# Mish from one Tanh and a polynomial instead of exponentials and reciprocals, and 56 instead of 47 sets of attention exponentials on VectorE

## The chip, the cores and the metric

The kernel runs on one core of one Trainium2 chip. A core has several engines that run at the same time, each with its own list of instructions: PE (TensorE, matrix products, with weight loads shown as PEld), ACT (ScalarE, tables of functions such as exp), DVE (VectorE, elementwise work), POOL (GpSimd) and SP (SyncE, which here only issues DMAs). An engine takes its instructions in order and waits at one until the semaphores that it needs are there.

The metric is the time of one execution on the device, in microseconds. Before the change the median of three runs is 902.22 us (902.0 to 902.47).

## What is computed

The input x has 2048 rows of 640. Two branches are mixed by a gate for each row: attention with 32 heads of 20 columns, and an MLP with the activation Mish.

```python
qkv = x @ wqkv                        # q, k, v: 32 heads of 20
scores = einsum("bhqd,bhkd->bhqk", q, k) * Dh ** -0.5
a = softmax(scores) @ v               # then @ wo
h = einsum("bsd,df->bsf", x, w1) + b1           # 640 -> 1536
sp = log1p(exp(-abs(h))) + where(h > 0, h, 0)   # softplus
b = einsum("bsf,fd->bsd", h * tanh(sp), w2)     # Mish, then 1536 -> 640
g = sigmoid((x * gate_w).sum(-1))
out = g * a + (1 - g) * b
```

The MLP takes x itself, as the attention does. Everything comes and goes as bf16.

## The kernel before

**Tiling.** The 2048 rows are four chunks `qc` of 512 queries, and the 32 heads are eight `p` of four heads each. A group G is one (p, qc): 32 groups in all, in the order of the list `groups`. In each group the keys are 16 tiles of 128. For a tile of keys and one head, PE makes a block of scores, 128 keys by 512 queries, in PSUM (L1150, tile `Sp`). The exponential of the block goes to SBUF (L1165, tile `E`), and a second product with the values adds it into `acc` (L1225), four heads at a time. One such step over four heads is called a set; a group has 16 sets. A column of ones beside the values gives the sum of the softmax, so that a group ends with a transpose, a reciprocal and a scaling on VectorE (`normalise`, L1185 to L1202).

**Iterations.** The blocks are handled in iterations that alternate between two score buffers: `S0` holds three blocks of 512 columns and `S1` two. One ACTIVATE takes the exponential of all the blocks in a buffer, so it has 1536 or 1024 columns. There are 819 iterations.

**Sets on VectorE.** Part of the sets have their exponential on VectorE. In such a case the third block of an `S0` buffer belongs to a VectorE set: `jv_read` (L794) rounds the block to int16 in one of the three ring buffers `E_dve`, and the ACTIVATE of that iteration takes only the 1024 columns left. After four such reads, one for each head, `jv_steps` makes the exponential of the set by seven steps on 128x2048 (L810 to L832): bits split into mantissa and exponent, a polynomial and an integer addition. The product for the set then reads `E_dve` and `VB`, a scaled copy of the last two tiles of values. `JV_SETS` says how many sets each group has on VectorE: two in the even groups and in group 31, one in the other groups from 1 on, 47 in all. `blocks` holds the place at which each read should come; within a group the reads are spread evenly.

**Mish.** `h_chain` makes `h` for one tile of 128 MLP columns and one chunk (L660, with the bias added at L670). For two tiles together (`mish_steps`, 24 times) ScalarE takes e = exp(h) (L589), and VectorE computes h * n / (n + 2) with n = e (e + 2). The division takes two fp32 reciprocals of 128x128 (L609) for 1024 columns: products of two and of four denominators are inverted and multiplied back (L599 to L618).

**What sets the order.** All instructions are written out in a fixed order by a planner in the kernel, which keeps estimates of each engine's time (`T`). Work other than scores, exponentials and set products is cut into chains with a start and a due iteration: projections of q, k and v, the MLP, the output projection (`wo_chain`, L739) and bounds that decide whether a fallback with maxima is needed. `pump` puts pieces of the chains between the scores of one iteration and those of the next, and fills PE with products of a constant (`busy_matmul`, L1090) where there is nothing else. VectorE's steps of Mish, of its sets and of `normalise` wait in the list `slow`, each with a deadline, and `run_slow` takes them by that deadline and avoids, where it can, two dependent steps behind each other.

**Ends of the groups.** Heads of pairs 0 to 5 are written to memory and fetched again (`fetch`) shortly before the output projection of their chunk. The last eight groups are, by chunk, pair 6 and pair 7. When pair 7 of a chunk is done, that chunk's output projection starts within the next group. Tiles of MLP activations and of heads share 40 buffers of 128x512 (`cells`).

SP issues the loads of w1, the weight strips and the heads; POOL issues the first loads and pads the q and k weights.

Of the kernel before, what the change touches and what calls it, by code (L numbers as in the profile page):

```python
# [2 lines left out]

# [147 lines left out]
def kernel(  # L151
# [12 lines left out]
    nc = tc.nc  # L164
    _, S, D = A_x.shape
# [7 lines left out]
    QC = 512  # L173
    NQC = S // QC
    NU = QC // P
    NQ = H // 4
# [2 lines left out]
    Q_SCALE = 512.0 * float(DH) ** -0.5 / LN2  # L179
    WIDTHS = (3, 2)  # L180

    JV_TWO = (*range(2, 31, 2), 31)
    JV_SETS = {G: 2 if G in JV_TWO else 1 for G in range(1, 32)}
    JV_RING = 3
    JV_AHEAD = 0.9
    JV_BIAS = 32
    N_CAP = 16382.0
    NCELL = 40
    MLP_FROM, MLP_TO = 10, 1
    CELLS_KEPT = 2  # L190

# [5 lines left out]
    consts = ctx.enter_context(tc.tile_pool(name="consts", bufs=1))  # L197
# [13 lines left out]
    mp = ctx.enter_context(tc.tile_pool(name="mp", bufs=1))  # L211
# [16 lines left out]
    cells = [consts.tile([P, QC], BF16, tag=f"cell{i}", name=f"cell{i}") for i in range(NCELL)]  # L228
    busy = consts.tile([P, P], BF16, tag="busy")
    xn = consts.tile([P, NQC], F32, tag="xn")  # L230
    wn = consts.tile([P, NQ, 2], F32, tag="wn")
    vn = consts.tile([P, 3], F32, tag="vn")
    F16, I16 = mybir.dt.float16, mybir.dt.int16
# [39 lines left out]
    warm = xn[:, 0:1]  # L273
    nc.vector.memset(warm, 0.0)
    nc.vector.memset(busy, 1.0)
    nc.scalar.activation(warm, warm, ACT.Exp)
    for t in (wqp[0], wkp[0], VA[:, :, :, DH : DH + 1], wqp[1], wkp[1], T2):
        nc.vector.memset(t, 1.0 if len(t.shape) == 4 and t.shape[-1] == 1 else 0.0)
    nc.gpsimd.dma_start(out=wv0[:, :, :], in_=wrows[:, :, 2 * D : 2 * D + 4 * DH])
    for c in range(1, NQC):  # L280
        nc.gpsimd.dma_start(
            out=xs[c][:, :, :],
            in_=x2d[c * QC : (c + 1) * QC, :].rearrange("(u p) d -> p u d", p=P),
# [4 lines left out]
        out=wv[:, :, GC : GC + 1], in_=gate_w.rearrange("(kt p o) -> p kt o", p=P, o=1)  # L288
# [14 lines left out]


    groups = [(p, qc) for p in range(NQ - 2) for qc in range(NQC)]
    groups += [(p, qc) for qc in range(NQC) for p in (NQ - 2, NQ - 1)]
    first = {}
    for G, (p, qc) in enumerate(groups):
        first.setdefault(p, G)


    units = []
# [6 lines left out]
    JV_START = {G: G - JV_AHEAD for G in range(34)}  # L319
    JV_START.update({1: 0.95, 25: 24.85, 32: 31.1})  # L320
    blocks = deque(
        (JV_START[G] + b * min(1.0, JV_START[G + 1] - JV_START[G]) / n, G, k, c)
        for G in JV_SETS
        for n in (4 * JV_SETS[G],)
        for b, (k, c) in enumerate((k, c) for k in range(JV_SETS[G]) for c in range(4))
    )
# [6 lines left out]
    while pos < len(units):  # L333
        i = len(iters)
        G = units[pos][0]
        n = min(WIDTHS[i % len(WIDTHS)], len(units) - pos)
        x = None
        far = G + (pos - unit_at[(G, 0)]) / (4.0 * (NS - JV_SETS.get(G, 0)))
        if n == 3 and blocks and blocks[0][0] <= far:
            _, g, k, slot = blocks[0]  # L340
# [3 lines left out]
            if left:  # L344
# [3 lines left out]
                n = 2  # L348
# [10 lines left out]
    def it_at(G, j=0):  # L359
        return it_of[unit_at[(G, j)]] if G < len(groups) else NI  # L360
# [218 lines left out]
    def mish_steps(m, c):  # L579


        h = h_of.pop((m, c))
        mish_free[0] = False
        e = mp.tile([P, 2 * QC], F32, tag="e", name="e")
        d = mp.tile([P, 4, 2 * P], F16, tag="d", name="d")
        d2 = mp.tile([P, 2, 2 * P], F32, tag="d2", name="d2")
        d4 = mp.tile([P, 2 * P], F32, tag="d4", name="d4")
        r2 = mp.tile([P, 2, 2 * P], BF16, tag="r2", name="r2")
        nc.scalar.activation(e[:, :], h[:, :, :].rearrange("p a n -> p (a n)"), ACT.Exp)  # L589
        T["act"] += NS_MISH_EXP  # L590
        V = nc.vector
        r = d2.rearrange("p a n -> p (a n)").bitcast(F16)
        y = d.rearrange("p a n -> p (a n)").bitcast(BF16)

        def n():
            V.scalar_tensor_tensor(out=e, in0=e, scalar=2.0, in1=e, op0=ALU.add, op1=ALU.mult)

        def products():
            V.tensor_scalar(  # L599
                out=d.rearrange("p a n -> p (a n)"), in0=e, scalar1=N_CAP, scalar2=2.0,  # L600
                op0=ALU.min, op1=ALU.add,
            )
            V.tensor_tensor(out=d2, in0=d[:, 0:2, :], in1=d[:, 2:4, :], op=ALU.mult)

        def invert(half):
            cols = slice(half * P, (half + 1) * P)
            if half == 0:
                V.tensor_tensor(out=d4, in0=d2[:, 0, :], in1=d2[:, 1, :], op=ALU.mult)
            V.reciprocal(out=d4[:, cols], in_=d4[:, cols])  # L609

        def of_two():
            V.tensor_tensor(
                out=r2, in0=d2[:, ::-1, :], in1=d4.unsqueeze(1).to_broadcast([P, 2, 2 * P]),
                op=ALU.mult,
            )

        def of_one():
            V.tensor_tensor(  # L618
                out=r.rearrange("p (b a n) -> p b a n", b=2, a=2),
                in0=d.rearrange("p (b a) n -> p b a n", b=2)[:, ::-1, :, :],  # L620
                in1=r2.unsqueeze(1).to_broadcast([P, 2, 2, 2 * P]),
                op=ALU.mult,
            )

        def share():
            V.scalar_tensor_tensor(out=y, in0=e, scalar=N_CAP, in1=r, op0=ALU.min, op1=ALU.mult)
            mish_free[0] = True

        def last(half):
            ft = 2 * m + half  # L630
            t = taken.pop((ft, c))
            V.tensor_tensor(out=t, in0=h[:, half, :], in1=y[:, half * QC : (half + 1) * QC], op=ALU.mult)
            act[(ft, c)] = t
            in_mish[0] -= half

        steps(
            T["act"] + 250.0,
            [
                (1217, n, True), (1415, products, True), (1400, lambda: invert(0), True),
                (947, lambda: invert(1), False), (692, of_two, True), (692, of_one, True),  # L640
                (1222, share, True), (420, lambda: last(0), True), (420, lambda: last(1), False),
            ],
            T["act"] + MISH_DUE,
            "mish",
        )
# [669 lines left out]
    half = QC // 2  # L1315
# [88 lines left out]
    for u in range(NU):  # L1404
        s = NU * last_qc + u
        ps = spool.tile([P, 2, QC], F32, tag=f"S{u % 2}", name="po")
        for half in range(2):
            nc.tensor.matmul(
                ps[:, half, 0:HALF],
                lhsT=OT[(NQ - 1, last_qc)][:, u * P : (u + 1) * P],  # L1410
                rhs=wo_sb[0][:, NQ - 1, half * HALF : (half + 1) * HALF],
                start=True,
                stop=True,
            )
        if u == 0:
            pair = mp.tile([P, 2, 2 * QC], BF16, tag="e", name="ot")
        if u < 2:
            ot = pair[:, u, :]
        else:
            ot = mp.tile([P, 2 * QC], BF16, tag=("d", "d2")[u - 2], name="ot")  # L1420
# [50 lines left out]
```

## Time and profile before

| | |
|---|---|
| median of three runs | 902.22 us |
| profiled execution, its time / its span | 902.6 / 900.8 us |
| ScalarE busy | 878.0 us, 97% |
| PE busy | 820.8 us, 91% |
| VectorE busy | 794.3 us, 88% |
| exponentials on ScalarE (L1165) | 819: 597 of 1024 and 222 of 1536 columns |
| reads of scores by VectorE (L794) | 188, 685 ns each |
| Mish exponentials on ScalarE (L589) | 24, 1142 ns each |
| granted clock of TensorE, mean | 0.996 |

The busy time of a group is the union of its instructions, so that it can be less than the number times the mean: neighbours overlap at their ends. Matmuls are pipelined, and a busy PE isn't PE at its peak. A group's line ends with the idle time of the engine just before its instructions, and with what ended that time (the releaser). "issue" is time in which the engine waited for nothing that the profile shows.

### The profile page before, as it was taken

How to read it: one execution, taken by the hardware profiler on the slowest of the kernel's cores; microseconds unless marked ns; L12 is line 12 of the kernel's file. 1: busy time of each engine (PE TensorE's matmuls, PEld its weight loads, DVE VectorE, ACT ScalarE, POOL GpSimd, SP SyncE). 2: the span in 40 equal slices, each digit the busy share in tenths (PEclk: the TensorE clock that was granted, in tenths of full speed). 3: DMA queues.
4: the chain of work that ended last, by engine and by line, in shares of the span. 5: the costliest groups of instructions: out<-in, count | busy, mean ns of one | idle time of the engine just before them, and what ended most of it. 6: DMA issues, size and time to landing. Idle time of an engine off the chain costs nothing.

```text
span 900.8 us, 14880 instructions
## 1 busy us (share of the span) xinstructions
PE 820.8 (91%) x5993; PEld 297.1 (33%) x6081; DVE 794.3 (88%) x1207; ACT 878.0 (97%) x849; POOL 25.3 (3%) x39
## 2 busy tenths in 40 slices
PE   8999898999998998989999989998999988999996
PEld 4443333233333333333333332333333333333332
DVE  4499999989989999989998999999999999988784
ACT  6999999999999999999999999999999999999994
POOL 5000010000000000000100000000000000000000
PEclk9999999999999999999999999999999999999998
DMA  9100010001000001000102000100001001110111
GB/s 264 36 7 22 21 31 1 21 22 31 7 21 15 21 7 30 22 19 32 31 28 51 8 21 15 31 36 21 21 16 43 27 1 40 44 44 8 50 53 39
DMA packets 37730, 28.27 MB, mean 31 GB/s; under 512 B 10984, under 2 KB 36472, under 8 KB 37656
## 3 DMA queue, kind: packets, MB, share of 16 engines
q1 hardware_dynamic: 34968, 20.90, 8.0%
q0 software_dynamic: 1456, 5.62, 2.1%
q8 instruction: 48, 0.79, 0.4%
q10 hardware_dynamic: 1232, 0.76, 0.3%
q14 instruction: 26, 0.21, 0.1%
HBM read 18.88 MB, written 8.39 MB: 30 GB/s over the span
## 4 chain that ended last, share of the span: by engine, by line
ACT 70%; PE 17%; issue 11%; DVE 2%; DMA 0%; ACTq 0%
ACT E L1165 67%; PE Sp L1150 5%; PE acc L1225 3%; ACT e L589 2%; PE ps L739 2%; PE ps L693 2%; PE ps L522 1%; PE ps L550 1%; PE ps L879 1%; DVE ot L1421 0%; DMA xs<-in_A_x_dram 0%; PE ps L660 0%; PE ps L480 0%; PE ps L1090 0%; PE ps L1301 0%
## 5 line engine op out<-in xcount | busy, mean ns | idle before, releaser
L1165 ACT ACTIVATE E<-Sp 128x1024 bf16<-128x1024 f32 (+1 forms) x819 | 856.6, 1232 | 3.9 <-PE Sp L1150 1.9
L1150 PE MATMUL Sp<-qT,kT 32*128 32x512 bf16 x2048 | 323.0, 382 | 61.5 <-ACT E L1165 44.7
L1150 PEld LDWEIGHTS <-kT 32*128 32x128 bf16 x2048 | 108.2, 91 | 284.6 <-issue 234.4
L1225 PE MATMUL acc<-E,VA 128*21 128x512 bf16 x1860 | 183.8, 386 | 0.0
L794 DVE TENSOR_SCALAR E_dve<-Sp 128x512 int16<-128x512 f32 x188 | 128.7, 685 | 31.7 <-PE Sp L1150 29.9
L1225 PEld LDWEIGHTS <-VA 128*21 128x21 bf16 x1860 | 45.6, 88 | 102.6 <-issue 102.4
L693 PE MATMUL ps<-w_sb,cell 128*128 128x320 bf16 x384 | 76.0, 303 | 0.2 <-issue 0.2
L1090 PE MATMUL ps<-busy 128*128 128x512 bf16 x229 | 71.2, 384 | 1.8 <-issue 1.6
L660 PE MATMUL ps<-xT,w1t 128*128 128x512 bf16 x215 | 71.2, 385 | 1.3 <-issue 1.3
L829 DVE TENSOR_TENSOR w_dve<-w_dve,u_dve 128x2048 bf16<-128x2048 f16 x47 | 57.1, 1215 | 0.2
L832 DVE TENSOR_TENSOR E_dve<-E_dve,w_dve 128x2048 int16<-128x2048 int16 x47 | 57.1, 1215 | 0.2
L820 DVE TENSOR_TENSOR w_dve<-w_dve 128x2048 f16<-128x2048 f16 x47 | 56.9, 1211 | 0.0
L739 PE MATMUL ps<-wo_sb,cell 128*128 128x320 bf16 x248 | 47.9, 302 | 0.0
L522 PE MATMUL ps<-xT,wkp 128*128 128x512 bf16 x135 | 43.3, 384 | 2.4 <-issue 1.4
L522 PE MATMUL ps<-xT,wqp 128*128 128x512 bf16 x137 | 43.9, 384 | 1.1 <-issue 0.9
L609 DVE RECIPROCAL d<-d 128x128 f32<-128x128 f32 x48 | 43.8, 934 | 0.8
L693 PEld LDWEIGHTS <-cell 128*128 128x128 bf16 x384 | 29.1, 97 | 35.4 <-issue 29.5
L670 DVE TENSOR_SCALAR h<-ps,b1f 128x512 bf16<-128x512 f32 x48 | 35.1, 731 | 0.8 <-PE ps L660 0.5
L810 DVE TENSOR_SCALAR w_dve<-E_dve 128x2048 int16<-128x2048 int16 x47 | 32.5, 692 | 1.2
L550 PE MATMUL ps<-wv,xT 128*128 128x80 bf16 (+2 forms) x240 | 33.3, 258 | 0.3 <-DVE xT L488 0.3
L815 DVE TENSOR_SCALAR E_dve<-E_dve 128x2048 int16<-128x2048 int16 x47 | 32.2, 686 | 1.1
L826 DVE TENSOR_SCALAR w_dve<-w_dve 128x2048 f16<-128x2048 f16 x47 | 32.1, 684 | 0.8
(105 smaller groups left out, 608.0 us busy)
## 6 DMA issues: line engine op xcount, KB each, us to landing
w1t<-in_B_w_dram SPq DMA_DIRECT2D x22, 320.0 KB, 3.1
heads_dram<-cell SPq DMA_DIRECT2D x24, 128.0 KB, 1.7
cell<-heads_dram SPq DMA_DIRECT2D x24, 128.0 KB, 2.9
b_dram<-Bt SPq DMA_DIRECT2D x4, 640.0 KB, 3.2
out_dram<-ot SPq DMA_DIRECT2D x14, 160.0 KB, 1.8
xs<-in_A_x_dram POOLq DMA_DIRECT2D x3, 640.0 KB, 7.1
w_sb<-in_B_w_dram POOLq DMA_DIRECT2D x1, 1920.0 KB, 12.6
ws<-in_A_wqkv_dram SPq DMA_DIRECT2D x13, 100.0 KB, 3.0
```

The lines of the kernel that those rows point to most:

```text
L522: nc.tensor.matmul(box["ps"][:, :], lhsT=wpad[:, kt, :, :].rearrange("p h d -> p (h d)"), rhs=xT[:, kt, chunk * QC : (chunk + 1) * QC], st ...
L660: nc.tensor.matmul(box["ps"][:, :], lhsT=w1t[NPAIR * c + m][:, kt, half * P : (half + 1) * P], rhs=xT[:, kt, c * QC : (c + 1) * QC], start ...
L693: nc.tensor.matmul(box["ps"][:, :], lhsT=act[(ft, c)][:, u * P : (u + 1) * P], rhs=w2_sb[:, ft, half * HALF : (half + 1) * HALF], start=(f ...
L739: nc.tensor.matmul(box["ps"][:, :], lhsT=OT[(p, c)][:, u * P : (u + 1) * P], rhs=wo_sb[0][:, p, cols], start=(k == 0), stop=(k == len(ps_l ...
L794: S_reader[0] = nc.vector.tensor_scalar(out=E_dve[ring].bitcast(I16)[:, slot, :], in0=ps, scalar1=ROUND, scalar2=ROUND - 512.0 * JV_BIAS, ...
L820: V.tensor_tensor(out=w, in0=w, in1=w, op=ALU.mult)
L829: V.tensor_tensor(out=w.bitcast(BF16), in0=w, in1=u, op=ALU.mult)
L832: V.tensor_tensor(out=e, in0=e, in1=wi, op=ALU.add)
L1090: nc.tensor.matmul(ps[:, 0:n], lhsT=busy[:, :], rhs=busy_row(n), start=True, stop=True)
L1150: nc.tensor.matmul(ps[:, k * QC : (k + 1) * QC], lhsT=kT[p][32 * t : 32 * t + 32, j * P : (j + 1) * P], rhs=qT[G][32 * t : 32 * t + 32, :] ...
L1165: exp = nc.scalar.activation(E[:, 0 : n * QC], S_of.pop(i)[:, 0 : n * QC], ACT.Exp, scale=LN2 / 512.0)
L1225: nc.tensor.matmul(acc[32 * t : 32 * t + DH + 1, :], lhsT=v, rhs=e, start=(n == 0), stop=(n == NS - 1), tile_position=(0, 32 * t),)
```

## The change

Four things are changed.

1. Mish: ScalarE takes T = tanh(h/2 + c) with c = log(0.4238062491)/2 from the tile `shift_t`, which VectorE fills once at the start. VectorE computes with S = T + 1: v = (S + A) S, then v * ((v + B)^2 + C) * K, all in fp16, and the product with h as before. Eleven VectorE instructions per pair of tiles become nine, and the reciprocals are gone. The planner's costs of the steps are changed with them.
2. VectorE has 56 sets instead of 47. They have one constant length, from place 0.95 to place 31.1 in units of groups, instead of one or two per group spread within it; a set belongs to the group that holds its end less 0.25. Group 1 has none, groups 5, 12, 19 and 26 have one each and the other groups to 31 two.
3. The last eight groups: pairs 6 and 7 of chunks 0 and 1 come as 6, 6, 7, 7, and those of chunks 2 and 3 chunk by chunk as before. The keys of pair 7 are projected over a longer stretch.
4. `cells` has 41 buffers instead of 40.

```diff
-    JV_TWO = (*range(2, 31, 2), 31)
-    JV_SETS = {G: 2 if G in JV_TWO else 1 for G in range(1, 32)}
+    JV_N, JV_FROM, JV_TO, JV_LATE = 56, 0.95, 31.1, 0.25
     JV_RING = 3
-    JV_AHEAD = 0.9
-    N_CAP = 16382.0
-    NCELL = 40
+    MISH_Z, MISH_A, MISH_B, MISH_C, MISH_K = (
+        0.4238062491, -3.9772710648, 1.0644427153, -50.2157789339, 0.00604176076620
+    )
+    NCELL = 41
...
+    nc.vector.memset(shift_t, math.log(MISH_Z) / 2)
...
-    groups += [(p, qc) for qc in range(NQC) for p in (NQ - 2, NQ - 1)]
+    groups += [(NQ - 2, 0), (NQ - 2, 1), (NQ - 1, 0), (NQ - 1, 1)]
+    groups += [(p, qc) for qc in range(2, NQC) for p in (NQ - 2, NQ - 1)]
...
+    set_length = (JV_TO - JV_FROM) / JV_N
+    JV_SETS = {}
+    blocks = deque()
+    for n in range(JV_N):
+        t = JV_FROM + n * set_length
+        G = min(max(1, math.ceil(t + set_length - JV_LATE)), len(groups) - 1)
+        k = JV_SETS.get(G, 0)
+        JV_SETS[G] = k + 1
+        t = max(t, G - 1.0)
+        blocks.extend((t + c * set_length / 4, G, k, c) for c in range(4))
...
-        nc.scalar.activation(e[:, :], h[:, :, :].rearrange("p a n -> p (a n)"), ACT.Exp)
+        nc.scalar.activation(
+            e[:, :], h[:, :, :].rearrange("p a n -> p (a n)"), ACT.Tanh, bias=shift_t[:, 0:1], scale=0.5
+        )
...
+        def one_more():
+            V.tensor_scalar(out=S, in0=e, scalar1=1.0, scalar2=None, op0=ALU.add)
+        def factor():
+            V.tensor_scalar(out=u, in0=S, scalar1=MISH_A, scalar2=None, op0=ALU.add)
+        def product():
+            V.tensor_tensor(out=v, in0=u, in1=S, op=ALU.mult)
+        def shifted():
+            V.tensor_scalar(out=u, in0=v, scalar1=MISH_B, scalar2=None, op0=ALU.add)
+        def square():
+            V.tensor_tensor(out=u, in0=u, in1=u, op=ALU.mult)
+        def factor2():
+            V.tensor_scalar(out=u, in0=u, scalar1=MISH_C, scalar2=MISH_K, op0=ALU.add, op1=ALU.mult)
+        def ratio():
+            V.tensor_tensor(out=S, in0=v, in1=u, op=ALU.mult)
...
-                (1217, n, True), (1415, products, True), (1400, lambda: invert(0), True),
-                (947, lambda: invert(1), False), (692, of_two, True), (692, of_one, True),
-                (1222, share, True), (420, lambda: last(0), True), (420, lambda: last(1), False),
+                (690, one_more, True), (427, factor, True), (692, product, True), (427, shifted, True),
+                (692, square, True), (427, factor2, True), (692, ratio, True),
+                (420, lambda: last(0), True), (420, lambda: last(1), False),
...
         if p == NQ - 1:
-            a, b = it_at(first[p] - 1) + 1, it_at(first[p]) - 4
+            a = it_at(first[p - 1]) + 1
```

More of the change, by code (lines that the diff above doesn't have):

```diff
@@ L1 @@
+import math
 from collections import deque
@@ L230 @@
     xn = consts.tile([P, NQC], F32, tag="xn")
+    shift_t = consts.tile([P, 1], F32, tag="shift_t")
     wn = consts.tile([P, NQ, 2], F32, tag="wn")
@@ L309 @@
         first.setdefault(p, G)
+    set_length = (JV_TO - JV_FROM) / JV_N
[8 more added lines that the diff above has]
+        blocks.extend((t + c * set_length / 4, G, k, c) for c in range(4))
+    assert max(JV_SETS.values()) <= 2
     units = []
@@ L318 @@
             units.extend((G, groups[G][0], groups[G][1], j, (j + k) % 4) for k in range(4))
[L319 to L326, printed above, removed]
     heads_of = {(G, k): [] for G in JV_SETS for k in range(JV_SETS[G])}
@@ L584, in mish_steps @@
         e = mp.tile([P, 2 * QC], F32, tag="e", name="e")
[L585 to L589, printed above, removed]
+        S = mp.tile([P, 2 * QC], F16, tag="y", name="S")
+        nc.scalar.activation(
+            e[:, :], h[:, :, :].rearrange("p a n -> p (a n)"), ACT.Tanh, bias=shift_t[:, 0:1], scale=0.5
+        )
@@ L590, in mish_steps @@
         T["act"] += NS_MISH_EXP
         V = nc.vector
[L592 to L623, printed above, removed]
@@ L625, in share @@
-        def share():
-            V.scalar_tensor_tensor(out=y, in0=e, scalar=N_CAP, in1=r, op0=ALU.min, op1=ALU.mult)
+        u, v = (e.bitcast(F16)[:, k * 2 * QC : (k + 1) * 2 * QC] for k in range(2))
+        def one_more():
[4 more added lines that the diff above has]
+            V.tensor_tensor(out=v, in0=u, in1=S, op=ALU.mult)
@@ L631, in last @@
             t = taken.pop((ft, c))
-            V.tensor_tensor(out=t, in0=h[:, half, :], in1=y[:, half * QC : (half + 1) * QC], op=ALU.mult)
+            V.tensor_tensor(out=t, in0=h[:, half, :], in1=S[:, half * QC : (half + 1) * QC], op=ALU.mult)
             act[(ft, c)] = t
@@ L1419 @@
         else:
-            ot = mp.tile([P, 2 * QC], BF16, tag=("d", "d2")[u - 2], name="ot")
+            ot = mp.tile([P, 2 * QC], BF16, tag=("d", "y")[u - 2], name="ot")
         nc.vector.scalar_tensor_tensor(
```

## The prediction

> **What bounds the kernel now.** I read the busy shares first, then the stages by window, then the groups of ScalarE and VectorE with shapes kept apart, then the waits, and the chain of work that ended last at the end of the span.
>
> The head of the page, and ScalarE and VectorE by stage. The columns of a window are its length, then busy us and count of PE, PEld, DVE, ACT, POOL, then the granted clock, DMA share and GB/s:
>
> ```profile
> span 900.8 us, 14880 instructions
> PE 820.8 (91%) x5993; PEld 297.1 (33%) x6081; DVE 794.3 (88%) x1207; ACT 878.0 (97%) x849; POOL 25.3 (3%) x39
> ...
> 100.00:200.00 100.00, 90.37 (x640) 31.58 (x648) 94.87 (x144) 99.90 (x100) 5.12 (x6) 1.00 0.07 20
> 300.00:400.00 100.00, 90.84 (x643) 32.22 (x652) 94.34 (x139) 100.00 (x98) 0.00 (x0) 1.00 0.06 17
> 600.00:700.00 100.00, 91.01 (x644) 30.95 (x653) 93.02 (x135) 100.00 (x98) 0.72 (x2) 1.00 0.08 23
> 800.00:880.00 80.00, 79.38 (x608) 29.55 (x606) 63.27 (x94) 78.78 (x75) 0.00 (x0) 1.00 0.12 38
> ```
>
> ScalarE (ACT) is busy 100 us of 100 in the middle: the kernel goes at its pace. VectorE is the next, 93 to 95. From 800 us on VectorE has room (63 of 80), but PE is as full as ScalarE.
>
> The groups by shape (busy, mean ns of one, idle before and its releaser):
>
> ```profile
> L1165 ACT ACTIVATE E<-Sp 128x1024 bf16<-128x1024 f32 x597 | 597.4, 1116 | 2.9 <-PE Sp L1150 1.0 <-PE acc L1225 0.3 <-ACT E L1165 0.2
> L1165 ACT ACTIVATE E<-Sp 128x1536 bf16<-128x1536 f32 x222 | 342.5, 1543 | 1.0 <-PE Sp L1150 0.8
> L794 DVE TENSOR_SCALAR E_dve<-Sp 128x512 int16<-128x512 f32 x188 | 128.7, 685 | 31.7 <-PE Sp L1150 29.9
> L820 DVE TENSOR_TENSOR w_dve<-w_dve 128x2048 f16<-128x2048 f16 x47 | 56.9, 1211 | 0.0
> L609 DVE RECIPROCAL d<-d 128x128 f32<-128x128 f32 x48 | 43.8, 934 | 0.8
> L826 DVE TENSOR_SCALAR w_dve<-w_dve 128x2048 f16<-128x2048 f16 x47 | 32.1, 684 | 0.8
> L596 DVE SCALAR_TENSOR_TENSOR e<-e 128x1024 f32<-128x1024 f32 x24 | 29.2, 1218 | 1.7 <-ACT e L589 1.7
> L589 ACT ACTIVATE e<-h 128x1024 f32<-128x1024 bf16 x24 | 27.4, 1142 | 0.2 <-DVE d L626 0.2
> L599 DVE TENSOR_SCALAR d<-e 128x1024 f16<-128x1024 f32 x24 | 16.7, 694 | 0.1
> L618 DVE TENSOR_TENSOR d<-d,r 128x1024 f16<-128x1024 f16 x24 | 16.5, 686 | 0.4
> ```
>
> An exponential of 1536 columns costs 1543 - 1116 = 427 ns more than one of 1024; the third 512 columns are what VectorE takes off ScalarE when it reads a block itself (L794). The 24 Mish exponentials are 3% of ScalarE. VectorE's reads wait for PE, 29.9 us in all, so VectorE still has slack there.
>
> The chain of work that ended last, at its end (start, us, what):
>
> ```profile
> 842.38 0.54 PE ps L739 x4
> 842.93 0.32 PE Sp L1150 x2
> 843.25 0.33 PE acc L1225 x4
> ```
>
> Between about 798 and 845 us this chain goes from score to score over PE, not over ScalarE: the output projection (L739) and the MLP's second product (L693) crowd PE there.
>
> **The change, part by part.** The sum is against the profiled execution's own 902.6 us (span 900.8); the median of the runs, 902.22, is 0.4 lower.
>
> *Nine more sets on VectorE (47 to 56).* A set is four heads of one 512-column block: 9 x 4 = 36 blocks. In the instruction order of the changed kernel 36 exponentials turn from 1536 to 1024 columns (222 to 186, 597 to 633); their total stays 819. On ScalarE: 36 x 427 ns = -15.4 us, on the path, since ScalarE is at 100%. The PV products change only their source (1860 and 188 become 1824 and 224): 0.
>
> *What nine sets cost VectorE.* One set: 4 reads at 685, four steps of 692, 686, 686 and 684, three of 1211, 1215 and 1215: 9.13 us; nine: +82.2 us.
>
> *Mish on VectorE.* Before, per pair of tiles: 1218 (L596) + 694 (L599) + 693 + 420 + 2 x 934 (L609) + 687 + 686 (L618) + 1216 + 2 x 416 = 8.31 us, x 24 = 199.5. After: one step from f32 to f16 at 694 (as L599); three products at 686 (as L618); three scalar steps on 1024 f16, a shape the trace lacks. L820 and L618 are the same operation at 2048 and 1024 columns, so the fixed part is 2 x 686 - 1211 = 161 ns, and a scalar step (684 at 2048) takes 161 + 523 / 2 = 422 ns; its bounds are 342 (half of L826) and 684 (no shorter at all), or +-6 us for 72 of them on VectorE. With the two closing products 694 + 3 x 686 + 3 x 422 + 2 x 416 = 4.85 us, x 24 = 116.4. Saved: 83.1 us. VectorE's work changes by -83.1 + 82.2 = -0.9 us: nothing. What covers it is ScalarE; without that cover 0.9 us is all there is to gain or lose.
>
> *But VectorE must do it in less time.* 794 us in a span 13 us shorter is 89.5% against 88%. Mish runs from 80 to 770 us, the sets all along, so the middle goes from some 94 to about 95%. Where VectorE comes late with a read (L794), PE cannot refill that score buffer and ScalarE waits. Before, starts of exponentials after a read lag no more (15 ns on average) than after none (16 ns); the bound below is 0. Above: I added VectorE's row times in the new order between one read and the next and set them against ScalarE's time for the same stretch. The mean run-ahead of VectorE goes from 0.21 to 0.36 us, with 2.1 us at most where it was 1.3. If all of ScalarE's mid-kernel lag grew with it (about 0.4 us in each 26 exponentials, 23 such stretches, x 0.36 / 0.21), it would be +6.6 us. I take +1.0, near the lower end, because reads cost nothing extra so far.
>
> *Short partners.* Start to start, an exponential of 1024 takes 904 ns and one of 1536 takes 1330 at the median. The one of the two-bank buffer that follows a short partner starts 45 ns late on average, after a long one 22. So 36 x 23 ns = +0.8 us (0 to 36 x 45 ns = 1.6).
>
> *Tanh with a per-partition bias (`shift_t`) in place of Exp.* Same columns, engine and place; the new order has one table load, as before. No ScalarE row has such an operand. VectorE's rows do: with `b1f` L670 takes 731 where L533 takes 686 with a constant, +45 ns. I take 50 ns x 24 = +1.2 us; ends 0 and, by the 203 ns that a ScalarE instruction on 128x1 takes in all (L276), 4.9. The Trainium skill, "ScalarE: Activation LUTs", section What ACT_TABLE_LOAD costs, gives about 93 ns for a [128,1] operand; by it this term would be an estimated 2.2 us and the sum 1.0 higher. No trace here shows it yet.
>
> *Order of the last groups.* Pair 7 of chunk 0 moves behind pair 6 of chunk 1, so the projection of chunk 0 comes one group later, and meets that of chunk 1 and the MLP's last products; pair 7's keys get one group more. In the new order PE's filler matmuls (L1090) vanish from exponentials 728 to 805, where nine stood (1.9 us). By the trace's start-to-start times a round of scores takes some 320 ns, a PV product 81, a product of 512 columns 226 and one of 320 columns 136. Counted so, PE's share of ScalarE's time in the three stretches of 26 from 728 on was 90, 100 and 90%, and becomes 100, 100 and 99%. ScalarE's lags there were 1.5, 2.7 and 0.8 us; at 2.7 for the first two and 2.0 for the third, 7.4 instead of 5.0: +2.4 us. Ends: 0 if PE absorbs it, and 5 if these stretches get twice the lag they had.
>
> *The rest.* ScalarE's wait for Mish's buffer (0.8 us over five places in its start times) ends as the chain shortens: -0.8. The memset of `shift_t` is behind the first loads: 0; uncovered it costs under 0.2 us. SP's 24 stores and 24 fetches of heads are the same number, some a group later; POOL's padding copies too: 0, covered by groups of 27 us. After the last exponential PE and VectorE have the same instructions: 0.
>
> Sum: 902.6 - 15.4 + 1.0 + 0.8 + 1.2 + 2.4 - 0.8 = 891.8; at the median's level (-0.4) about 891.4 us.
>
> **Rivals.**
> 1. *The full gain.* The even pace of sets takes away the places where reads bunch, and PE absorbs the end: 902.2 - 15.4 = 886.8. For it: reads are not late today. Against: PE's crowded end. Chance 0.23.
> 2. *VectorE is tight and hands back part.* Run-ahead turns into lag as in the upper bound (+6.6), the bias at 4.9: 891.4 + 5.6 + 3.7 = 900.7 with both, about 897 with the first. For: 95% in the middle. Chance 0.18.
> 3. *Slower: VectorE becomes the bound.* Place: Mish's six f16 steps. If these ran at one column per cycle, as the f32 step L596 does (1218), they would add 24 x (3 x 796 + 3 x 532) = 96 us to VectorE; the middle would stand at 95 x (1 + 96 / 794) = 106%, and the time at about 902 x 1.06 = 956 less VectorE's free ends (some 35 us): near 920. It decides once Mish takes over 45 us more than the 116. Against: L826 and L618 run f16 at the rates used. Chance 0.04.
> 4. *Slower: table switches.* If Tanh needed another table, 48 loads of 1283 ns (the one ACT_TABLE_LOAD row) on the bound engine: 891.4 + 61.6 = 953. Against: one load in the new order. The Trainium skill, "ScalarE: Activation LUTs", section Table sets, puts exp and tanh in one set, and so agrees. Chance 0.02.
> 5. *Moves nothing.* PE paces more than the end, and the 36 shorter exponentials only wait: about 902. Against: 217 fillers stay in PE's order, 49 us at 226 ns. Chance 0.03.
>
> **How the numbers follow.** The forecast, 891.4, has 0.50. A tenth of a per cent either way is noise; 0.2% (1.8 us) is about what can be told from no change. Faster: 0.50 + 0.23 + 0.18, less 0.01 of the second rival beyond 900.4, = 0.90; same 0.03 + 0.01 = 0.04; slower 0.06. The range runs from rival 1 less a little for reads that stop bunching (886.0) to past rival 2's usual value (898.5): outside lie rivals 3 to 5 (0.09) and the edges of 1 and 2 (about 0.09).
>
> **What would show it.** L1165 as x633 at about 1116 and x186 at 1543; ScalarE at 99 to 100% in the middle; the sum of VectorE's busy time within 5 us of 794; the f16 steps near 420 and 686 ns; Tanh's mean 1142 to 1240 with one ACT_TABLE_LOAD. The lag of exponentials 728 to 805 should be about 7 us, where it was 5. I am wrong if VectorE's reads stop waiting for PE and PE waits for E_dve much over 15.7 us, if f16 steps take over 600 ns, or if the chain runs over PE before 700 us.

## The result, and the profile after

The changed kernel takes 892.57 us (median of four runs, 891.85 to 895.23), the kernel before 902.35 in runs beside it: a ratio of 0.9895, with a 95% interval of 0.9872 to 0.9918. The forecast was 891.4 in a range of 886.0 to 898.5. Runs of one kernel are longer where the mean granted clock is lower (for the kernel before 901.4 to 903.0 us at 0.996, 905 to 906 at 0.99), so a time called "at full clock" below is that of runs at 0.995 or more.

The profiled execution of the changed kernel took 892.05 us, 10.55 less than that of before (902.6). The head of its page, and the same four windows, the last one 10 us shorter; the columns are the length, busy us and count of PE, PEld, DVE, ACT and POOL, the granted clock, the DMA share and GB/s:

```profile
span 890.3 us, 14943 instructions
PE 825.0 (93%) x6044; PEld 288.6 (32%) x6044; DVE 788.3 (89%) x1259; ACT 866.2 (97%) x849; POOL 25.3 (3%) x39
...
100.00:200.00 100.00, 91.48 (x666) 31.55 (x663) 92.34 (x150) 98.75 (x99) 4.58 (x6) 1.00 0.07 18
300.00:400.00 100.00, 92.82 (x665) 31.85 (x661) 95.14 (x149) 99.89 (x100) 0.00 (x0) 1.00 0.07 21
600.00:700.00 100.00, 93.59 (x651) 30.55 (x652) 93.35 (x144) 99.88 (x100) 0.00 (x0) 1.00 0.07 21
800.00:870.00 70.00, 69.88 (x545) 25.95 (x542) 58.67 (x88) 68.71 (x66) 0.00 (x0) 1.00 0.12 38
```

ScalarE is still the pace: 99.9 of 100 in two of the windows, 98.75 in the first, for which a reason is found below. VectorE's share hardly moves, 92 to 95 where it was 93 to 95: Mish gave it room, and the nine sets took the room back.

The groups by shape, of the changed kernel (busy, mean ns of one, idle before and its releaser):

```profile
L1160 ACT ACTIVATE E<-Sp 128x1024 bf16<-128x1024 f32 x633 | 624.2, 1123 | 5.1 <-PE acc L1220 2.0 <-PE Sp L1145 1.0
L1160 ACT ACTIVATE E<-Sp 128x1536 bf16<-128x1536 f32 x186 | 286.2, 1539 | 0.9 <-PE Sp L1145 0.8
L789 DVE TENSOR_SCALAR E_dve<-Sp 128x512 int16<-128x512 f32 x224 | 153.9, 687 | 31.7 <-PE Sp L1145 29.0
L595 ACT ACTIVATE e<-h,shift_t 128x1024 f32<-128x1024 bf16 x24 | 30.1, 1252 | 0.0
L615 DVE TENSOR_TENSOR e<-e 128x1024 f16<-128x1024 f16 x24 | 16.6, 690 | 0.4
L603 DVE TENSOR_SCALAR S<-e 128x1024 f16<-128x1024 f32 x24 | 16.5, 689 | 5.4 <-ACT e L595 5.2
L606 DVE TENSOR_SCALAR e<-S 128x1024 f16<-128x1024 f16 x24 | 10.2, 423 | 0.2
L618 DVE TENSOR_SCALAR e<-e 128x1024 f16<-128x1024 f16 x24 | 10.3, 427 | 0.6
```

The 633 and 186 are as counted. Mish's new steps take 689, 423, 690 and 427 ns, where 694, 422, 686 and 422 stood in the sum. The mean duration of an exponential of 1024 went from 1116 to 1123, but durations of neighbours overlap. What counts on a full engine is the distance from one start to the next. That is 904 ns at the median for 1024 columns and 1330 for 1536, in both kernels to 1 ns. For the exponential of Mish it went from 947 ns to 1040 for the Tanh.

With these medians ScalarE's time can be cut into three parts: the medians themselves, what starts beyond them (the *lag* of an instruction), and the ends. The 10.55 us come out so:

| part | forecast | measured |
|---|---|---|
| 36 exponentials from 1536 to 1024 columns | -15.4 | -15.3 (36 x 426) |
| Tanh with an operand instead of Exp, x 24 | +1.2 | +2.2 (24 x 93) |
| lag, exponentials 728 to 805 | +2.4 | +1.1 (5.0 to 6.1) |
| lag elsewhere (reads +1.0, short partners +0.8, Mish's buffer -0.8) | +1.0 | +2.0 (15.3 to 17.3) |
| before the first exponential and after the last | 0 | -0.6 (10.7 to 10.4, 11.9 to 11.6) |
| sum | -10.8 | -10.6 |

Of the 2.0 us of lag elsewhere, 1.7 lie in one stretch of 26 exponentials, from number 130 (0.4 to 2.1 us), and one event makes 1.0 of them. The chain of work that ended last, in the changed kernel, passes through VectorE there (start, us, what):

```profile
151.33 0.69 DVE E_dve L789
152.02 1.14 DVE E_dve L827
153.16 0.02 issue
153.19 0.71 DVE w_dve L805
153.89 0.02 issue
153.91 0.69 DVE E_dve L810
154.61 0.64 DVE T L1180
155.24 0.04 issue
155.29 0.39 PE acc L1220
```

VectorE had waited 0.85 us for the scores of its read (L789). In its order stood behind the read a last step of one set, two first steps of the next, and only then the transpose that closes the group (L1180). PE may not write the next group's `acc` before that transpose; the scores stand behind that product in PE's order; and ScalarE runs out of scores. The wait is the 1.0 us in this line of ScalarE's waits (us in total, times, longest):

```profile
ACT E L1160 <- PE acc L1220: 2.0, 6, 1.0
```

### The profile page after: what moved, and what is told of

Same layout as the page of the kernel before. It is cut to its first block, busy times and chain, and to the rows that moved or that the text cites. A ratio compares the mean times of both kernels' runs of the same rounds, so it can differ in the third digit from the quotient of the medians.

```text
span 890.3 us, 14943 instructions
## 1 busy us (share of the span) xinstructions
PE 825.0 (93%) x6044; PEld 288.6 (32%) x6044; DVE 788.3 (89%) x1259; ACT 866.2 (97%) x849; POOL 25.3 (3%) x39
## 4 chain that ended last, share of the span: by engine, by line
ACT 65%; PE 21%; issue 9%; DVE 4%; DMA 0%; ACTq 0%
ACT E L1160 62%; PE Sp L1145 7%; PE acc L1220 4%; PE ps L734 4%; ACT e L595 3%; PE ps L688 2%; PE ps L530 2%; PE ps L655 1%; PE ps L558 1%; DVE E_dve L789 1%; DVE E_dve L827 1%; PE ps L874 1%; DVE ot L1416 0%; DMA xs<-in_A_x_dram 0%; DVE w_dve L805 0%
## 5 line engine op out<-in xcount | busy, mean ns | idle before, releaser
L1160 ACT ACTIVATE E<-Sp 128x1024 bf16<-128x1024 f32 (+1 forms) x819 | 843.3, 1217 | 6.0 <-PE acc L1220 2.0
L789 DVE TENSOR_SCALAR E_dve<-Sp 128x512 int16<-128x512 f32 x224 | 153.9, 687 | 31.7 <-PE Sp L1145 29.0
L827 DVE TENSOR_TENSOR E_dve<-E_dve,w_dve 128x2048 int16<-128x2048 int16 x56 | 68.4, 1221 | 0.3
L824 DVE TENSOR_TENSOR w_dve<-w_dve,u_dve 128x2048 bf16<-128x2048 f16 x56 | 68.2, 1218 | 0.4
L815 DVE TENSOR_TENSOR w_dve<-w_dve 128x2048 f16<-128x2048 f16 x56 | 67.9, 1213 | 0.0
L1085 PE MATMUL ps<-busy 128*128 128x512 bf16 (+1 forms) x217 | 66.7, 382 | 0.0
L530 PE MATMUL ps<-xT,wkp 128*128 128x512 bf16 x155 | 49.6, 384 | 0.8 <-DVE xT L496 0.8
L810 DVE TENSOR_SCALAR E_dve<-E_dve 128x2048 int16<-128x2048 int16 x56 | 38.6, 689 | 1.2
L821 DVE TENSOR_SCALAR w_dve<-w_dve 128x2048 f16<-128x2048 f16 x56 | 38.5, 688 | 1.0
L818 DVE TENSOR_SCALAR u_dve<-w_dve 128x2048 f16<-128x2048 f16 x56 | 38.3, 684 | 0.4
```

Source lines behind the costliest of these rows:

```text
L530: nc.tensor.matmul(box["ps"][:, :], lhsT=wpad[:, kt, :, :].rearrange("p h d -> p (h d)"), rhs=xT[:, kt, chunk * QC : (chunk + 1) * QC], st ...
L789: S_reader[0] = nc.vector.tensor_scalar(out=E_dve[ring].bitcast(I16)[:, slot, :], in0=ps, scalar1=ROUND, scalar2=ROUND - 512.0 * JV_BIAS, ...
L815: V.tensor_tensor(out=w, in0=w, in1=w, op=ALU.mult)
L824: V.tensor_tensor(out=w.bitcast(BF16), in0=w, in1=u, op=ALU.mult)
L827: V.tensor_tensor(out=e, in0=e, in1=wi, op=ALU.add)
L1085: nc.tensor.matmul(ps[:, 0:n], lhsT=busy[:, :], rhs=busy_row(n), start=True, stop=True)
```

## The experiments

**What paces the kernel: each half of the change alone.** The theory is that ScalarE paces it, so that a faster Mish gives nothing by itself and the sets give everything. The rival is that VectorE already paces part of the middle, so that Mish gives something by itself. The first run puts the new Mish into the kernel before, with 47 sets and the old order:

```diff
-        nc.scalar.activation(e[:, :], h[:, :, :].rearrange("p a n -> p (a n)"), ACT.Exp)
+        nc.scalar.activation(
+            e[:, :], h[:, :, :].rearrange("p a n -> p (a n)"), ACT.Tanh, bias=shift_t[:, 0:1], scale=0.5
+        )
...
-                (1217, n, True), (1415, products, True), (1400, lambda: invert(0), True),
-                (947, lambda: invert(1), False), (692, of_two, True), (692, of_one, True),
-                (1222, share, True), (420, lambda: last(0), True), (420, lambda: last(1), False),
+                (690, one_more, True), (427, factor, True), (692, product, True), (427, shifted, True),
+                (692, square, True), (427, factor2, True), (692, ratio, True),
+                (420, lambda: last(0), True), (420, lambda: last(1), False),
```

> The kernel before with the new Mish alone (Tanh and polynomial; 47 sets, their places and the order of the groups as before). VectorE loses some 83 us of work, ScalarE nothing. Theory A (ScalarE paces, VectorE is covered): the 24 Tanh cost 93 ns more each, +2.2 us, and the waits for Mish's buffer end, -0.8 us: about 903.8 us, between 902.5 and 905. Rival V (VectorE paces, or shares the pace): a tenth less VectorE work gives a large gain, under 895 us.

Measured: 903.4 to 903.8 us at full clock, against some 902.2 for the kernel before; the ratio over all runs, 1.0018 [0.9985, 1.0052], alone would not tell the two apart. The head of its page:

```profile
span 901.9 us, 14813 instructions
...
PE 816.5 (91%) x5985; PEld 294.0 (33%) x6070; DVE 716.2 (79%) x1160; ACT 879.2 (97%) x849; POOL 26.0 (3%) x39
```

VectorE works 78 us less, and the kernel is not faster but a microsecond slower: the Tanh costs 2.2 us more, the first exponential starts 0.8 earlier, and the lag stays (20.2 us for 20.3). The rival falls.

The second run is the other half: the even sets and the new order, but the old Mish, 40 buffers, and 50 sets. Against the changed kernel (the lines of Mish, which are those of the kernel before, are left out):

```diff
-    JV_N, JV_FROM, JV_TO, JV_LATE = 56, 0.95, 31.1, 0.25
+    JV_N, JV_FROM, JV_TO, JV_LATE = 50, 0.95, 31.1, 0.25
...
-    NCELL = 41
+    NCELL = 40
```

> The changed kernel with the old Mish (Exp, reciprocals) and 50 sets instead of 56, at the constant pace and with the new order of groups. 50 is the most for which the planner finds room beside the old Mish. Against the kernel before 12 exponentials lose 512 columns: -5.1 us on ScalarE; VectorE gets 27 us more (some 821). Theory A: a gain less than the 5.1, since the reads come late more often and PE is fuller at the end: 898 to 900 us. Rival V: VectorE's 27 us show, 910 us or more.

Measured: 939.6 us (937.9 to 941.4), ratio 1.0369 [1.0291, 1.0446]. The theory's 898 to 900 was far off. VectorE's instructions sum to 882 us where the kernel before has 855: 27 us more VectorE work cost 37 us, in runs whose clock (0.983 to 0.990) was lower too. The windows of this kernel, and its chain behind the last exponential, show where:

```profile
700.00:800.00 100.00, 94.32 (x661) 31.46 (x665) 87.83 (x138) 95.53 (x92) 0.00 (x0) 0.97 0.11 34
800.00:900.00 100.00, 92.26 (x676) 33.49 (x683) 94.31 (x137) 96.49 (x92) 0.00 (x0) 1.00 0.12 37
900.00:940.00 40.00, 24.83 (x154) 15.79 (x154) 20.46 (x33) 0.00 (x0) 0.00 (x0) 0.78 0.10 34
```

```profile
896.91 1.07 ACT e L596
...
898.00 1.24 DVE e L603
...
901.17 1.77 DVE d L616 x2
...
904.42 1.24 DVE d L633
...
906.16 14.80 PE ps L700 x86
920.96 7.62 PE ps L746 x56
```

The attention ends at 896 us, 7 later than before (888.9), as the lag grows from 20.3 to 35.4 us. Above all, Mish comes after the sets in VectorE's list of deadlines; its last exponential starts at 896.9 us, where that of before starts at 769.4, and the MLP's second product (L700) and the output projection (L746) run alone behind it: 43.6 us after the last exponential, where there were 11.9. So with these deadlines the lighter Mish is what makes room for the sets, and neither half gained anything alone. Whether the old Mish, ordered ahead of the sets, would leave a part of the gain was not tried.

**The Tanh's operand.** The same kernel with the constant in the instruction:

```diff
-            e[:, :], h[:, :, :].rearrange("p a n -> p (a n)"), ACT.Tanh, bias=shift_t[:, 0:1], scale=0.5
+            e[:, :], h[:, :, :].rearrange("p a n -> p (a n)"), ACT.Tanh, bias=math.log(MISH_Z) / 2, scale=0.5
```

> The changed kernel with the bias of Tanh as a constant of the instruction instead of the per-partition tile. Theory A (the operand costs the 93 ns that Tanh's start-to-start distance grew by): Tanh's mean falls from 1252 to about 1150 ns and the time from 892.6 by 2.2 us to about 890.3 us. Rival T (Tanh itself is slower than Exp): mean stays near 1250, time stays at 892.6 us.

Measured: 890.6 us (889.73 to 891.63), 889.7 and 890.0 at full clock; ratio to the kernel before 0.9838 [0.9766, 0.9909]. The group of this kernel:

```profile
L595 ACT ACTIVATE e<-h 128x1024 f32<-128x1024 bf16 x24 | 27.9, 1164 | 0.0
```

Start to start is 947 ns again. The lag agrees with that of the changed kernel in every stretch to 0.1 us (23.4 in all), the single event included, and the profiled execution is 2.3 us shorter: 24 x 93 ns and nothing else. It is the fastest kernel of the study.

**The order of the groups.** Only the new order of the last eight groups and pair 7's longer stretch, in the kernel before:

```diff
-    groups += [(p, qc) for qc in range(NQC) for p in (NQ - 2, NQ - 1)]
+    groups += [(NQ - 2, 0), (NQ - 2, 1), (NQ - 1, 0), (NQ - 1, 1)]
+    groups += [(p, qc) for qc in range(2, NQC) for p in (NQ - 2, NQ - 1)]
```

> The kernel before with the new order of the last groups and the longer stretch for the keys of pair 7 alone. By its instruction order PE's share in the three stretches of 26 exponentials from 728 on goes from 90, 100 and 90% to 98, 100 and 95%. Theory A: their lag grows from 5.0 to about 6.5 us, time about 903.9 us, between 903 and 905. Rival P0 (PE absorbs the crowd): 902.4 us within 0.5. Rival P1 (the new order is what makes the end cheaper): under 901.5 us.

Measured: 904.05 and 904.25 at full clock (+1.9), 907.8 over all ten runs, ratio 1.0017 [0.9978, 1.0057]. The time is the expected one, but its place isn't shown: the profiled execution, one at a lower clock, has a lag of 5.4 us in exponentials 728 to 805, 0.4 more than before, and another 5.8 in a stretch in which TensorE's clock was halved.

**Fewer sets, and the even pace.** With the new Mish and order, 52 sets and 47 sets:

```diff
-    JV_N, JV_FROM, JV_TO, JV_LATE = 56, 0.95, 31.1, 0.25
+    JV_N, JV_FROM, JV_TO, JV_LATE = 52, 0.95, 31.1, 0.25
```

> The changed kernel with 52 sets. 16 exponentials get 512 columns more on ScalarE: 16 x 427 ns = +6.8 us; VectorE gets 36 us less. Theory A (ScalarE paces): 898.5 to 900 us where the granted clock is undisturbed. Theory F in its strong form (VectorE is the bound with 56 sets): less VectorE work pays back, under 896 us.

> The changed kernel with 47 sets: new Mish, new order of groups, the even pace, but the number of sets as before. Against the run with the new Mish alone (903.6 undisturbed) only order and pace differ. Theory A (the pace is worth nothing, the order costs 1.9 us as it did alone): about 905.5 us. Rival (the even pace is itself a gain): under 903 us.

With 52 sets 898.5 us in the one run at full clock (median 900.65, ratio 0.9989 [0.9972, 1.0007]): 6.5 above the changed kernel's 892.05 for 16 blocks at 426 ns, 6.8. So from 52 to 56 a set is still worth its whole price: the lag is 23.3 us with 52 and 23.4 with 56. With 47 sets 902.6 to 904.3 at full clock (median 904.1, ratio 1.0012 [0.9998, 1.0027]): around the 903 of one expectation and under the 905.5 of the other, and about the 903.4 to 903.8 of the run with Mish alone, from which it differs in pace and order. Outside exponentials 728 to 805, and without one stretch that the profile shows at half clock, its lag is 13.3 us against 15.7: the even pace saves about 2 us. Inside them it is 5.4 against 4.2: the order costs about 1. From 47 to 52 sets, though, the time falls by 4.0 to 5.8 us at full clock for 20 blocks at 426 ns, 8.5, and the lag rises from 19.0 us (without the half-clock stretch's excess) to 23.3: these five sets gave half to two thirds of their price, by one run of 52 sets at full clock and one profiled execution of each kernel.

**How much more can VectorE take.** The changed kernel with Mish's first product done twice, and four times; the same result is written again, so that only VectorE's work grows, by 16.3 and 49.8 us:

```diff
             V.tensor_tensor(out=v, in0=u, in1=S, op=ALU.mult)
+            V.tensor_tensor(out=v, in0=u, in1=S, op=ALU.mult)
```

> The changed kernel with one of Mish's products made twice (same values), 24 more VectorE instructions of 685 ns, some 15 us of VectorE in all, unknown to the planner, so that the order of everything else stays. After the run of 50 sets beside the old Mish, which ended at 939.6 us with the MLP left over behind the attention, the theory is: VectorE at 95% of the middle is nearly full (theory F: its idle 5% is mostly gaps between dependent steps), so that added work shows to more than half: 900 to 908 us. Rival C (VectorE is still covered by ScalarE, its waits for PE, 29 us, are real slack): 893 to 896 us.

> The same with the product made four times: some 47 us more VectorE. Theory F: nearly all of it shows, 925 to 940 us. Rival C: the first 25 to 30 us vanish in waits for PE, the rest shows: 905 to 918 us.

Twice: 899.7 us (898.4 to 899.9 at full clock), ratio to the kernel before 0.9968 [0.9951, 0.9984]: between the two expectations, close under the 900 of theory F. The profiled execution is 7.8 us longer than that of the changed kernel, and the lag grows by just that, 23.4 to 31.2: about half of the added work shows. Four times: 996.6 us (993.4 to 1000.6 in three runs; a fourth, at a mean clock of 0.864, took 1024.6), ratio 1.1059 [1.1012, 1.1106]. That is 104 us for 50, twice what was added, and outside both expectations. The page and waits of this last kernel, with a window from its middle:

```profile
span 991.6 us, 15015 instructions
...
PE 897.5 (91%) x6044; PEld 286.6 (29%) x6044; DVE 839.3 (85%) x1331; ACT 881.4 (89%) x849; POOL 26.4 (3%) x39
...
400.00:500.00 100.00, 91.90 (x560) 25.27 (x558) 86.97 (x133) 86.76 (x85) 4.74 (x4) 0.82 0.08 23
```

```profile
ACT E L1163 <- PE Sp L1148: 75.7, 104, 1.9
DVE E_dve L792 <- PE Sp L1148: 60.9, 78, 3.0
PEld L1148 <- DVE E_dve L792: 58.7, 69, 2.7
```

No engine is full. VectorE waits for PE's scores, PE for VectorE's reads, and ScalarE for PE. In a fixed order a late read doesn't stop one engine but all three. The granted clock is 0.82 to 0.91 in four windows between 100 and 880 us, so PE is slower as well. How the 104 us divide between the waits and the clock isn't settled: each feeds the other. The first sign stands already in the kernel with the product twice, whose score loads wait 43.9 us for the reads, where those of the changed kernel (the second line) wait 18.5:

```profile
PEld L1146 <- DVE E_dve L790: 43.9, 91, 1.3
PEld L1145 <- DVE E_dve L789: 18.5, 56, 0.6
```

**Toward a faster kernel.** The best kernel above has the constant bias. Four kernels meant to go below it failed. One more set with an earlier end of the MLP (`MLP_TO` says how many groups before the last one the MLP's chains are due), to empty the crowded end:

```diff
-    JV_N, JV_FROM, JV_TO, JV_LATE = 56, 0.95, 31.1, 0.25
+    JV_N, JV_FROM, JV_TO, JV_LATE = 57, 0.95, 31.1, 0.25
...
-    MLP_FROM, MLP_TO = 10, 1
+    MLP_FROM, MLP_TO = 10, 2
```

> The changed kernel with the constant bias, 57 sets (the most for which the planner finds room) and the MLP planned one group earlier. ScalarE: 4 blocks fewer than with 56 sets, -1.7 us from the 889.9 of the constant bias; VectorE: +9 us, and Mish is denser. PE's crowded stretches move from 728-805 to 702-779, their shares are 100, 100, 95 and 82% where they were 87, 100, 100 and 99%. Theory F (VectorE nearly full, half of what is added shows): -1.7 + 4 and some us for PE's end, 890 to 894 us. Rival C (VectorE is covered): 887 to 889 us.

Measured: 896.0 us (890.7 and 891.3 at full clock), ratio 0.9911 [0.9884, 0.9938]. The crowd moved rather than went: the lag of exponentials 702 to 805 is 6.6 us where it was 6.3.

The others put the f32 step of Mish on GpSimd, to take 16.5 us off VectorE, with 56 sets, with 58, and with 57 and the earlier MLP (the planner then starts the other steps 4 us later):

```diff
-        def one_more():
-            V.tensor_scalar(out=S, in0=e, scalar1=1.0, scalar2=None, op0=ALU.add)
+        nc.gpsimd.tensor_scalar(out=S, in0=e, scalar1=1.0, scalar2=None, op0=ALU.add)
```

> The changed kernel with the constant bias, and with Mish's first step (T + 1, from f32 to f16) on GpSimd, which is 97% idle: 24 x 694 ns = 16.7 us less on VectorE, 56 sets as before. The mirror of the run with 16 us more on VectorE, which cost 7 us. Theory F: the lag of the exponentials outside PE's crowded ends, some 15 us, falls by 2 to 4 us: 886 to 888 us. Rival C (VectorE is covered): 889.9 within 0.7. Rival G (GpSimd and VectorE hinder each other): over 891 us.

> The same with 58 sets, which spend the time that VectorE got back (+18.3 us): 8 blocks fewer on ScalarE, -3.4 us against the constant bias (889.9), VectorE as full as with 56 sets and the step on VectorE. Theory A with F: 886 to 887.5 us. Rival G: over 890 us.

> Step on GpSimd, constant bias, 57 sets, MLP planned one group earlier. ScalarE -1.7 us against 889.9; VectorE 7 us less than there; the crowd on PE is spread over four stretches instead of three. Theory A with F: 885.5 to 888 us, and a lag of the exponentials 702 to 805 of 6 us or less. Rival: the earlier MLP only moves the crowd, lag there 6.5 us as with it late (6.3 in 702 to 805).

Measured: 909.5 us, ratio 1.0073 [1.0048, 1.0099], with 56 sets; 898.8, ratio 0.9979 [0.9953, 1.0005], with 58; 909.8 to 912.3 in four runs and 933.1 in a fifth at a mean clock of 0.949, ratio 1.009 [1.0073, 1.0107], with 57. All are slower than the kernel with the constant bias. The group and two waits of the first of them:

```profile
L602 POOL TENSOR_SCALAR S<-e 128x1024 f16<-128x1024 f32 x24 | 73.2, 3052 | 641.7 <-ACT e L595 605.4 <-DVE cell L626 19.3 <-DMA ws<-in_A_wqkv_dram 17.0
```

```profile
POOL S L602 <- ACT e L595: 27.5, 1, 27.5
PE ps L530 <- POOL wkp L303: 3.1, 1, 3.1
```

Most of the loss goes with TensorE's clock. The first of them is 19.8 us longer in its profiled execution than the kernel with the constant bias, its lag is 19.9 us more, and 18.0 of these lie in the four stretches of 26 exponentials around its three pieces at half clock (0.50, from 346, 674 and 759 us). What set the clock off there is shown for one piece only. Two things show besides. First, a step that takes VectorE 689 ns takes GpSimd 3052, and while it runs VectorE's scalar steps of the sets take 1066 ns on average (19 of 224 overlap) where they take 690 otherwise. VectorE's instructions sum to 850.1 us where 840.2 was due (856.7 less 16.5), so 10 of the 16.5 us come back. The Trainium skill, "GPSIMD Engine Reference", section Key points, says that GpSimd shares its memory interfaces with VectorE; the longer steps agree. Second, GpSimd works in order too: the copies that pad a pair's weights (L303) stood behind a Mish step that waited 27.5 us for its Tanh, and PE stood 3.1 us for them; its clock was 0.50 right after.

## Why the prediction was right

*Nine more sets, 36 x 427 ns.* Right, as the counts, the start-to-start medians and the run with 52 sets show.

*Mish's price and the balance on VectorE.* Right. The prices of shapes that the trace lacked, from two points of another shape, were within 6 ns (419 to 427 for 422, 680 to 690 for 686 and 689 for 694). One bound of these prices was worked out wrongly: 72 scalar steps at 684 ns instead of 422 would have been 18.9 us more, not 6. VectorE's durations sum to 855.3 us before and 856.7 after, where -0.9 was worked out. The busy time fell 6.0 us, one more than the 5 given as a sign, since it counts overlaps once.

*Tanh.* Mis-sized: this term of the sum was +1.2 and measured +2.2. Its price came from another engine's rows (45 ns more on VectorE), and ScalarE's is 93 ns. The mean duration, 1252, lies past the 1142 to 1240 given as a sign. The Trainium skill, "ScalarE: Activation LUTs", section What ACT_TABLE_LOAD costs, gave about 93 ns, and the trace agrees with it to the nanosecond. One table load stayed (rival 4 falls).

*The order of the last groups.* The place was right, the size half: exponentials 728 to 805 lag 6.1 us where 7.4 stood in the sum. PE is the bound there as predicted; the chain of the changed kernel goes over PE from product to product:

```profile
844.54 0.38 PE ps L734 x2
...
845.24 0.33 PE acc L1220 x4
...
846.13 0.79 PE ps L734 x5
```

The counted shares of 100, 100 and 99% gave less lag (2.1, 2.5 and 1.6 us by stretch) than the 2.7, 2.7 and 2.0 taken from the one stretch that stood at 100% before.

*VectorE late with reads.* The sum took +1.0 for it and +0.8 for short partners. What the runs give instead is about +4.4 us from 47 to 56 sets at the even pace, by the lag (19.0 without the half-clock stretch's excess, to 23.4), all of it between 47 and 52, with about -2 us for the even pace against it. That second term stood in no line of the sum; it was only an argument of rival 1. The two together come near the +1.8. The largest single piece wasn't a late read but a late transpose behind a read, a wait that the forecast didn't name. Reads that end over 300 ns after ScalarE's own part went from 2 of 188 to 4 of 224.

*Rivals.* The full gain (886.8) fell to the Tanh, PE's end and the lag. Rival 2, near 897, did not come about, but 16 us more on VectorE bring the kernel to 898.4 to 899.9, so the edge that it warned of is near. Rivals 3 to 5 did not come about either: the f16 steps took the times above, there is one table load, and the time moved. But rival 3 was priced wrong: it took VectorE's overload as additive, deciding only beyond 45 us more. The two runs with added products show half the addition at 16 us and twice at 50, and the run with the old Mish shows a third form of it, the MLP left over at the end. The errors of the sum, +1.0, -1.3, +1.0 and -0.6, nearly cancel; it is 0.2 us off in total with single terms off by more than 1. That the total is so close is luck; that the gain is near 10 us is not, since the term of 15.4 held to 0.1 us.

*Signs of being wrong.* None came: the scalar f16 steps took 419 to 427 ns, VectorE's reads still wait 29.0 us for PE, PE's score loads wait 18.5 us for the reads where 15.7 stood, and from 100 to 700 us the chain lies on ScalarE for most of its length, with short pieces over PE such as the one at 155 us.

## What to carry to other kernels

Work freed on an engine that isn't the bound is room and no gain: price it by what the room lets you move off the bound, and count how full the engine is afterward, best by adding known work to it: in the fixed order here 78 us less on VectorE gained nothing, 16 us more showed to half, and 50 us more showed twice. On the bound engine, price each operand by that engine's own rows, and use a constant in the instruction where one will do. A helper engine that shares a resource with the one it relieves, or has other work in its queue, gives back part of what it takes. And where the time moves, look at the granted clock before the engines.

## What the hardware showed that was not expected

Short gaps in PE came with long stretches at half clock. In the profiled executions of the kernel before, the changed kernel, Mish alone, the constant bias and 52 sets, no window of 4 us from 12 to 872 us has a granted clock under 1.00. The other nine have stretches, mostly of 8 to 20 us, at 0.50 (windows that they fill in part read up to 0.78), and the 26 exponentials around one mostly have 2 to 8 us of lag or more. PE before one of them, in the kernel with constant bias and 57 sets, and the windows behind it:

```profile
451.89 0.39 PE L1145 MATMUL Sp<-qT,kT 32*128 32x512 bf16 x3 [0.53 <-ACT E L1160]
454.15 0.42 PE L1145 MATMUL Sp<-qT,kT 32*128 32x512 bf16 x3 [0.90 <-ACT E L1160]
```

```profile
455.00:460.00 5.00, 5.00 (x24) 0.88 (x20) 3.72 (x7) 3.14 (x5) 0.00 (x0) 0.50 0.09 28
460.00:465.00 5.00, 4.67 (x22) 0.88 (x19) 3.06 (x6) 3.92 (x4) 0.00 (x0) 0.50 0.00 0
...
475.00:480.00 5.00, 4.65 (x37) 1.85 (x34) 4.90 (x7) 5.00 (x5) 0.00 (x0) 1.00 0.55 88
```

PE waits twice for ScalarE, 0.53 and 0.90 us within three microseconds; then the clock is halved for 20 us, though PE is busy for all but 0.3 of them, and ScalarE falls to 3.1 to 3.9 of 5.

Gaps alone don't settle it: the changed kernel's 0.9 us wait at 154 us left the clock at 1.00. A grid does. In each trace the changes of the clock lie a whole number of steps of 3.41 us apart; in this one the stretches begin at 454.40, 751.36 and, at the end of the kernel, 891.30 us, 87 and 41 steps apart. Every trace has such a change at its end, so each can be cut by its grid. From 20 to 872 us, the 14 traces have 34 windows at full clock with such a stretch right behind them, and PE is idle for at least 1.32 us in 33 of these (1.14 in the other). In the 3352 windows at full clock without one it is idle for less than 1.30, but for two (1.33 and 1.39). The last window before the stretch above and the first in it:

```profile
450.98:454.39 3.41, 1.98 (x15) 0.75 (x15) 3.38 (x8) 3.41 (x4) 0.00 (x0) 1.00 0.00 0
454.39:457.81 3.42, 3.42 (x19) 0.65 (x16) 2.67 (x5) 2.57 (x3) 0.00 (x0) 0.50 0.14 43
```

And the wait at 154 us, in the changed kernel (first line) and with Mish's product twice:

```profile
152.01:155.42 3.41, 2.36 (x22) 0.79 (x20) 3.34 (x6) 2.79 (x3) 0.00 (x0) 1.00 0.00 0
154.86:158.27 3.41, 1.85 (x19) 0.58 (x17) 3.34 (x7) 2.29 (x3) 0.00 (x0) 1.00 0.00 0
158.27:161.68 3.41, 3.41 (x15) 0.69 (x13) 2.41 (x4) 2.82 (x3) 0.00 (x0) 0.50 0.02 7
```

PE's idle time is the length less its busy time: 1.43 and 1.56 us before a halving, 1.05 without. So the traces fit a clock that goes by PE's idle time summed within one window of the grid, with the edge near 1.3 us of 3.41; this is inferred from the counts, and no run set out to test it. The Trainium skill, "TensorE: Matmul & The Clock Gate", section What's actually happening, has the clock halved after an idle window of about 3.4 us, and restored after one as long that is busy. Here the length of the window agrees, but a window idle for 1.1 to 3.2 us was enough and the recovery took up to twelve windows, and the measurement decides. Its section A second HAM failure mode: psum-queue depth-cycling has frequent short idle times do the same, without a length; the trace agrees with that.

Why the clock comes back after one window in some cases and after six in this one stays open; so does why runs of one kernel differ in their mean clock. The grid is a candidate, not shown: in the profiled execution of Mish alone PE is idle for 1.85 us of the 3.41 from 757.15, but its grid cuts this into windows of 0.84 and 1.29, and the clock stays at 1.00. A run in which the grid lies otherwise would have it in one.
